# A weight sum behind the token sums, one store per quadrant and another order of the last products, in a linear attention and mixture-of-experts kernel

## The chip, the cores and the metric

The kernel runs on one core of one Trainium2 chip. The metric is the device time of one execution in microseconds (us). The core has five engines with a queue each: TensorE (PE in the profile), VectorE (DVE), ScalarE (ACT), GpSimd (POOL) and SyncE (SP, which only issues DMAs). ScalarE and GpSimd issue DMAs too. Each queue runs in order; the queues wait for one another by semaphores.

## The reference

Attention with a feature map phi replaces the softmax, for 8 samples, 8 heads, 576 tokens and 64 features per head. Its output, 4608 tokens of 512 features, goes through four experts whose outputs are added with a weight per token:

```python
kv = np.einsum('bhsd,bhse->bhde', k_p, v)
num = np.einsum('bhsd,bhde->bhse', q_p, kv)
...
for e in range(E):
    h = np.maximum(x @ w1[e], 0.0)
    out += p[:, e:e + 1] * (h @ w2[e])
```

Each expert has a first layer of 512 by 1024 and a second of 1024 by 512. The result is float32; the kernel multiplies in float16.

## The kernel before

**Tiles.** Tokens are worked on in nine tiles of 512. Tile j, from 0 to 7, is the first 512 tokens of sample j. The ninth tile, j = 8, holds the 64 tokens left over of each of the eight samples; its input is the tile `xT_left`. A unit is one tile and one expert; `81`, `82`, `83` in a name stand for tile 8 with experts 1, 2, 3.

**Products.** From tile 1 on, both layers use seven products in place of eight for a two-by-two block product (a Strassen scheme). It needs sums: of weights (`weight_sums`, `weight_sums2`, on VectorE, once per expert, lines 742 to 767), of input tokens (`token_sum`, on GpSimd, names `ts`, line 847) and of hidden values (`hidden_sum`, on GpSimd, names `hs`, lines 776 to 782). `t2.0` is `weight_sums2(2, 0)`, line 761: the difference of two blocks of the second-layer weights of expert 2, 128 partitions by 1024 elements. `t2.1` reads its result.

**A block of the first layer** (class `Block`) has the steps p1, p2, p6, p7, p5, c22, p4, p3. Products (line 866) go into the accumulators `b` and `e` in PSUM; ScalarE copies or applies ReLU (lines 877, 892, 899, 920); VectorE adds a copy and applies ReLU (`add_relu`, line 850).

**The second layer** (`layer2_product`, line 809) takes two halves of tokens (i = 0, 1) and seven products p. Each is four matmuls of 128 by 256. `m83.61` is product 6, second half, of tile 8 and expert 3. Products 1, 6, 7, 4 add up in one accumulator (`run`), 2, 5, 3 in another (`side`, which 2 and 5 start anew). After each product VectorE adds the accumulator, times the token's weight, into the float32 tile `acc` (`add_acc`, line 705), so the next product into the same accumulator waits for that add. For most units `run` and `side` are halves of a `py` bank; for the very last unit they are the banks `b` and `e`. In tile 0 the second layer is done plainly, in pieces y (line 714): `y2.33` is the last piece of expert 2 for the fourth group of 128 tokens.

**Stores.** An `acc` tile has 128 tokens by 512 features. For j < 8 SP stores it as one DMA (line 686). For the last tile, 64 of the 128 rows belong to each of two samples, whose rows lie 576 apart in DRAM. A quadrant (128 rows, 256 features) is stored as soon as it is done, after products 2, 7, 3 and 4, by two DMAs of 64 rows (line 692): one on SP's queue and one on ScalarE's, and for product 7, second half, both on GpSimd's.

**Order.** The order of all work is written out. Until about 100 us it is the list `EARLY` of names; each occurrence advances a step to its next `yield`. In the part around 70 us are `ts1.3` and `ts1.2` (token sums of tile 1), `b2.lkm` (line 385, two VectorE passes over left-over keys, tile `kz`), `b2.lq` (line 376 on ScalarE, which needs the PSUM that `b2.lkm` read) and `b1.load3` (an SP load). After `EARLY` each step has a position number, and steps run whole in order of it; the last unit's products use the order (1, 2, 6, 5, 7, 3, 4). At the end the order on TensorE is m82.70, .71, .40, .41, then m83.10, .11, .20, .21, .60, .61, .50, .51, .70, .71, .30, .31, .40, .41.

Of the kernel before, what the change touches and what calls it, by code (L numbers as in the profile page):

```python
# [80 lines left out]
    "KC": ('VV', 'VA', 'AA', 'AV'),  # L81
    "XT": ('AA', 'VV', 'VA', 'VV'),
    "CUT": (((0, 3, 4), (0, 3, 4), (0, 4), (0, 4)), ((0, 2, 4),) * 4),
    "WARM": (14, 5, 3, 1, 2, 1, 1),
    "BANK": {'qT0': 'b', 'qT1': 'py', 'kv2': 'py', 'qT2': 'py', 'kv3': 'b', 'nd10': 'b', 'nd10+': 'py', 'nd00': 'py', 'xT20': 'b', 'nd01': 'b', 'xT00': 'b', 'xT10': 'py', 'xT30': 'py', 'nd11': 'b', 'L20': 'b', 'xT11': 'b', 'L30': 'e', 'L10': 'e', 'L11': 'e', 'L00': 'py', 'L31': 'b', 'L01': 'e', 'L21': 'py', 'b1.lk': 'py', 'b1.q1': 'py', 'b1.q3': 'b', 'b1.q0': 'py', 'b1.nd10': 'b', 'b1.qT0': 'py', 'b1.nd00': 'b', 'b1.xT0': 'b', 'b1.xT3': 'py', 'b1.qTl': 'py', 'b1.nl': 'py'},
    "EARLY": (
# [12 lines left out]
        "p4.030 p2.031 b1.qT1 p6.031 p4.030 b1.nd21 w230 b1.qT0 b1.nd20 p7.031 c22.030 p5.031 b1.qT0 b1.nd00 b1.xT3 s3.2 b1.nd20 b1.nd01 b1.qT1 p3.030 b1.xT2",  # L99
        "b1.nd00 b1.nd10 b1.nd01 y2.20 b1.xT3 b1.nd11 y2.21 b2.ones p7.031 b1.xT2 b1.lq b1.xT0 y2.22 y2.23 b1.xT0 b1.nd10 b1.nd11 b1.xT1 b1.xT1 b2.load1 y2.02",  # L100
        "y2.03 ts1.0 b1.load4 b2.k0 p4.031 p4.031 b1.load1 p1.101 y2.30 p3.030 y2.23 p1.101 ts1.1 b2.lk c22.031 p3.031 y2.03 p1.100 b1.lqm y2.31 b1.qTl w231",
        "p1.100 p6.101 b1.qTl ts1.3 p3.031 b2.load0 y2.32 y2.33 b1.load3 t2.0 b2.lv p2.101 p6.100 p6.100 y2.33 b2.lkm y2.10 y2.11 t2.1 t0.1 b2.lq p2.100 p2.100",
        "y2.12 y2.13 b2.v0 p2.101 t3.0 b2.load5 p6.101 ts1.2 p7.100 y3.20 p7.100 b2.k3 y3.21 b2.v1 b2.load2 p5.100 p7.101 p7.101 b2.k1 b2.load3 y2.13 b1.nl",
        "y3.22 b2.km0 c22.100 b1.nl y3.23 b2.km3 y3.23 p3.100 p3.100 p4.100 b2.load9 p4.100 p5.101 b2.v2 b2.k2 b2.lqm y3.23 y3.10 y3.00 y3.01 p4.101 y3.02",
        "y3.03 p1.110 b2.km1 p4.101 hs10.00 t1.1 b2.v3 y3.11 p1.110 p6.110 c22.101 y3.03 b2.load4 b2.km2 p2.110 b2.kv p6.110 p2.110 y3.12 y3.13",
# [17 lines left out]
def kernel(  # L123
# [10 lines left out]
    nc = tc.nc  # L134
    ATTN, HSUM, L2ORD, L2AT = (CFG[x] for x in ("ATTN", "HSUM", "L2ORD", "L2AT"))

    B, H, S, D = q.shape
    N, E = moe_domain_probs.shape
    _, Dm, F = moe_w1.shape

    P = 128
    HP = P // 2
    CM = S // P
    SM = CM * P
# [67 lines left out]
    out_b = out.rearrange("(b s) d -> b s d", s=S)  # L212
# [467 lines left out]
    def new_py():  # L680
        return ppm.tile([P, Dm], FP32, tag="py", bufs=2, name="py")

    def store(j, ns, cols=slice(0, Dm), engs=(nc.sync, nc.scalar)):
        acc = accs[j, ns][:, cols]
        if j < B:
            nc.sync.dma_start(
                out=out_b[j, 0:SM].rearrange("(p c) d -> c p d", c=CM)[ns],
                in_=acc,
            )
        else:  # L690
            for u in range(2):
                engs[u].dma_start(
                    out=out_b[2 * ns + u, SM:S, cols],
                    in_=acc[u * HP : (u + 1) * HP],
                )

    def add_acc(j, e, ns, ps, ds, first):
        if (j, ns) not in accs:
            accs[j, ns] = pm.tile([P, Dm], FP32, tag="acc", bufs=NACC, name="acc")
        acc = accs[j, ns][:, ds]  # L700
        pscal = p_sb[:, j, ns, e : e + 1]
        if first:
            nc.scalar.activation(acc, ps, AF.Identity, scale=pscal)  # L703
        else:
            nc.vector.scalar_tensor_tensor(  # L705
                out=acc, in0=ps, scalar=pscal, in1=acc, op0=AO.mult, op1=AO.add
            )
# [76 lines left out]
    def layer2_product(j, e, hT, hss, p, i):  # L784


        if (j, e) == (NTILES - 1, E - 1):
            if p == 1:
                pys[j, e, i] = [ppm.tile([P, DH], FP32, tag=tag, bufs=2, name=f"p{tag}") for tag in ("b", "e")]
            run, side = pys[j, e, i]  # L790
        else:
            if p == 2:
                pys[j, e, i] = new_py()
            run, side = pys[j, e, i][:, 0:DH], pys[j, e, i][:, DH:Dm]
        ts = slice(i * P, (i + 1) * P)
        ts2 = slice(NH + i * P, NH + (i + 1) * P)
        w, tw = w2_sb[e], t2_sb[e]
        lo, hi = slice(0, FH), slice(FH, FC)
        ps, lhsT, rhs, first = {
            1: (run, lambda k: hT[k // 2][:, k % 2, 0, ts], w[:, lo, 0:DH], (j, e) == (NTILES - 1, E - 1)),  # L800
            2: (side, lambda k: hT[k // 2][:, k % 2, 1, ts], w[:, hi, 0:DH], True),
            5: (side, lambda k: hss[k // 2][0][:, k % 2, ts], tw[:, 0], True),
            6: (run, lambda k: hss[k // 2][1][:, k % 2, ts], tw[:, 1], False),
            7: (run, lambda k: hT[k // 2][:, k % 2, 0, ts2], w[:, lo, DH:Dm], False),
            3: (side, lambda k: hss[k // 2][3][:, k % 2, ts], w[:, hi, DH:Dm], False),
            4: (run, lambda k: hT[k // 2][:, k % 2, 1, ts2], tw[:, 2], False),
        }[p]
        for k in range(FH):
            nc.tensor.matmul(  # L809
                out=ps,  # L810
                lhsT=lhsT(k),
                rhs=rhs[:, k],
                start=first and k == 0,
                stop=k == FH - 1,
                skip_group_check=True,
            )
        yield
        c1, c2 = slice(0, DH), slice(DH, Dm)
        ns, ds, first = {
            2: (i, c1, True),  # L820
            5: (2 + i, c2, True),
            1: (i, c1, False),
            6: (i, c2, True),
            7: (2 + i, c2, False),
            3: (i, c2, False),
            4: (2 + i, c1, True),
        }[p]
        add_acc(j, e, ns, ps, ds, first and e == 0)
        if (j, e) == (NTILES - 1, E - 1):
            if p in (2, 3, 4, 7):  # L830
                yield
                store(j, ns, ds, *([(nc.gpsimd,) * 2] if (p, i) == (7, 1) else ()))
        elif e == E - 1 and p in (3, 4):
            yield
            store(j, ns)
# [164 lines left out]
    b0, b1 = bts[0], bts[1]  # L1000
    on = {"A": nc.scalar, "V": nc.vector, "P": nc.gpsimd, "S": nc.sync}
    with tc.manual_schedule(
# [5 lines left out]
        work = []  # L1008

        def put_at(pos, name, *g):  # L1010
            work.append((pos, len(work), name, g))
# [24 lines left out]
        NSLOT, LAG = 7, 6  # L1036

        def put_block(at, *g):
            bl = Block(*g)
            for pos, name in ((0, "p1"), (3, "p2"), (5, "p6"), (8, "p7"), (9, "p5"), (9.1, "c22"), (11, "p4"), (13, "p3")):  # L1040
                put_at(at + pos, f"{name}.{g[0]}{g[1]}{g[2]}", getattr(bl, name))
# [18 lines left out]
        for n, (j, e) in enumerate(units):  # L1060
            h, hss = [None, None], [[None] * 4, [None] * 4]
            at = base + 2 * NSLOT * n
            for d in range(2):
                put_block(at + d * NSLOT, j, e, d, h)
            at += 2 * NSLOT + LAG

            def hsum(d, i, hT=h, hss=hss):
                hidden_sum(hT[d], hss[d], i)

            for d in range(2):  # L1070
                for i in range(4):
                    put_at(at + HSUM[d][i], f"hs{j}{e}.{d}{i}", hsum, d, i)
            order = L2ORD
            if n == len(units) - 1:
                order, at = (1, 2, 6, 5, 7, 3, 4), at + NSLOT
            for m in range(14):
                put_at(at + L2AT[m], f"m{j}{e}.{order[m // 2]}{m % 2}", layer2_product, j, e, h, hss, order[m // 2], m % 2)

        for j in range(0, NTILES - 1):
            at = base + 2 * NSLOT * E * (j - 1) if j else 0.0  # L1080

            def put(pos, *g, at=at):
                put_at(at + pos, *g)

            if j + 1 < B:
                nxt = bts[j + 2] if j + 2 < B else None
                batch_steps(bts[j + 1], nxt, put, ATTN[j > 0], ATTN[1])
            else:
                put(CFG["LATE"][0], "b0.alloc", b0.alloc_left)
                put(CFG["LATE"][0], "b0.load", b0.load_left, "q")  # L1090
                put(CFG["LATE"][1], "b0.lq", b0.left_act, "q")
                put(CFG["LATE"][2], "b0.lqm", b0.left_dve, "q")
                put(CFG["LATE"][2] + 1, "b0.qTl", b0.dma_qTl)
                put(CFG["LATE"][3], "b0.nl", b0.nd_left)
            for i in range(4):
                if j:
                    put(2 * NSLOT * E + CFG["TSUM"][i], f"ts{j + 1}.{i}", token_sum, j + 1, i)
                else:
                    put(base + CFG["TSUM1"][i], f"ts1.{i}", token_sum, 1, i)
        work.sort(key=lambda w: w[0:2])  # L1100
        live = {name: g for _, _, name, g in work}
        assert len(live) == len(work)
# [45 lines left out]
```

## Time and profile before

| what | value |
|---|---|
| median of 3 runs | 491.01 us (491.0 to 491.03) |
| profiled execution | 491.24 us, its span 489.5 us |
| granted TensorE clock | 0.998 |
| HBM | 45.16 MB read, 9.44 MB written |
| second-layer matmul, 128x256 (L809) | one per 0.109 us, four in 0.44 us |
| add into acc, 128x256 (L705) | 0.48 us, one per 0.437 us in a row |
| hidden or token sum on GpSimd | 1.15 to 1.17 us |
| weight sum, 128x1024 (L761), four of them | 683, 688 (median) to 3419 ns |
| issue of a 64-row store on SP (L692) | 0.47 to 0.56 us |
| its landing after the issue | 1.9 to 2.6 us |

The span runs from the first to the last instruction in the trace; some 1.7 us lie around it. A line of the profile names the source line, the engine, what is written and read, the shapes, and how many instructions were merged. An idle time in brackets names what ended it. A queue's name with a q (SPq, ACTq) stands for the issuing of DMAs.

### The profile page before, as it was taken

Reading aid. Unit: us, or ns where it says so; the run is one execution under the profiler, and the core shown is the slowest. Engines: PE = TensorE matmul, PEld = TensorE weight load, DVE = VectorE, ACT = ScalarE, POOL = GpSimd, SP = SyncE. Lnnn points to the kernel's source line nnn. Section 1 sums busy time; section 2 is a strip of 40 time slices with the busy share of each in tenths; the row PEclk is TensorE's granted clock in tenths of the full one; section 3 lists DMA queues with packets and bytes.
Section 4 is the critical chain, followed back from the end, with each engine's and each line's share of the span. In section 5 each row is a group of like instructions: output and inputs, shape, how many; then the busy total and the mean of one; then the engine's idle time right before and its main releaser. Section 6 shows DMA issues by size and latency. Waiting matters only on the chain.

```text
span 489.5 us, 12007 instructions
## 1 busy us (share of the span) xinstructions
PE 477.5 (98%) x4567; PEld 407.8 (83%) x4567; DVE 382.2 (78%) x801; ACT 330.8 (68%) x656; POOL 358.3 (73%) x341
## 2 busy tenths in 40 slices
PE   7899998999999999999999999999999999999996
PEld 3676665898888988898889888988898888888885
DVE  5768999998958886788769885978687756775686
ACT  5489979855896498748884888478954565446530
POOL 4655044688967896789776976697769877987775
PEclk9999999999999999999999999999999999999999
DMA  8999968532445235524552345423131020002003
GB/s 280 199 226 262 249 127 243 154 94 47 134 154 122 50 112 190 113 60 113 171 128 65 95 144 145 92 56 119 56 76 28 5 95 1 2 0 88 2 1 86
DMA packets 81017, 53.67 MB, mean 110 GB/s; under 512 B 45152, under 2 KB 73696, under 8 KB 80960
## 3 DMA queue, kind: packets, MB, share of 16 engines
q1 hardware_dynamic: 70512, 41.05, 30.7%
q0 software_dynamic: 9888, 11.41, 12.3%
q8 instruction: 35, 0.57, 0.5%
q10 hardware_dynamic: 560, 0.46, 0.3%
q14 instruction: 22, 0.18, 0.1%
HBM read 45.16 MB, written 9.44 MB: 112 GB/s over the span
## 4 chain that ended last, share of the span: by engine, by line
PE 91%; ACT 3%; DVE 2%; DMA 1%; issue 1%; SPq 0%; DVEq 0%; ACTq 0%
PE py L809 39%; PE pb L866 24%; PE pe L866 18%; PE py L714 4%; PE ph L654 1%; PE psum_nd L471 1%; DMA kraws<-in_k_dram 1%; PE psum_kv L443 1%; DVE acc L705 1%; PE pb L809 1%; PE pe L809 0%; DVE t L761 0%; PE psum_nl L489 0%; ACT kp L343 0%; ACT u L877 0%
## 5 line engine op out<-in xcount | busy, mean ns | idle before, releaser
L705 DVE SCALAR_TENSOR_TENSOR acc<-py,p_sb,acc 128x256 f32<-128x256 f32 (+1 forms) x382 | 181.7, 488 | 43.1 <-PE py L809 37.3
L850 DVE CUSTOM_DVE_ANT_0 h<-pe,u 128x512 f16<-128x512 f32 x140 | 96.0, 687 | 46.8 <-PE pe L866 27.1
L866 PEld LDWEIGHTS <-w 128*128 128x128 f16 x1120 | 109.1, 98 | 17.4 <-issue 1.3
L776 POOL TENSOR_TENSOR hs<-h 128x512 f16<-128x512 f16 x64 | 73.9, 1154 | 59.4 <-DVE h L850 57.5
L809 PEld LDWEIGHTS <-h 128*128 128x128 f16 x1024 | 99.6, 98 | 12.7 <-issue 1.2
L809 PE MATMUL py<-w,h 128*128 128x256 f16 x744 | 106.4, 273 | 0.6 <-ACT acc L703 0.6
L877 ACT COPY u<-pb 128x512 f32<-128x512 f32 x140 | 82.5, 592 | 32.4 <-PE pb L866 29.7
L778 POOL TENSOR_TENSOR hs<-hs,h 128x512 f16<-128x512 f16 x64 | 75.0, 1173 | 26.4 <-PE py L809 24.0
L866 PEld LDWEIGHTS <-s 128*128 128x128 f16 x840 | 81.4, 98 | 12.1 <-issue 1.1
L866 PE MATMUL pb<-tt,w 128*128 128x256 f16 x560 | 83.7, 273 | 0.9 <-ACT u L877 0.9
L809 PEld LDWEIGHTS <-hs 128*128 128x128 f16 x768 | 74.4, 98 | 8.9 <-POOL hs L776 0.2
L782 POOL TENSOR_TENSOR hs<-h,hs 128x512 f16<-128x512 f16 x64 | 74.7, 1168 | 0.9 <-PE py L809 0.3
L780 POOL TENSOR_TENSOR h<-h 128x512 f16<-128x512 f16 x64 | 74.8, 1168 | 0.2
L809 PE MATMUL py<-t,hs 128*128 128x256 f16 x496 | 74.3, 273 | 0.0
L899 ACT ACTIVATE h<-pe 128x512 f16<-128x512 f32 x70 | 42.0, 600 | 44.1 <-PE pe L866 40.7
L892 ACT COPY pe<-pb 128x512 f32<-128x512 f32 x70 | 40.1, 574 | 38.6 <-PE pb L866 14.1
L920 ACT ACTIVATE h<-pb 128x512 f16<-128x512 f32 x70 | 42.0, 600 | 7.0 <-PE pb L866 7.0
L866 PE MATMUL pb<-tt,s 128*128 128x256 f16 x280 | 41.8, 272 | 0.6 <-ACT pe L892 0.6
L866 PE MATMUL pe<-tt,s 128*128 128x256 f16 x280 | 41.9, 273 | 0.0
L866 PE MATMUL pe<-xT,s 128*128 128x256 f16 x248 | 37.3, 273 | 0.0
L866 PE MATMUL pe<-xT,w 128*128 128x256 f16 x248 | 37.2, 273 | 0.0
L866 PE MATMUL pb<-xT,w 128*128 128x256 f16 x248 | 37.0, 273 | 0.0
(133 smaller groups left out, 598.7 us busy)
## 6 DMA issues: line engine op xcount, KB each, us to landing
out_dram<-acc SPq DMA_DIRECT2D x32, 256.0 KB, 2.5
w<-in_moe_w_dram POOLq DMA_DIRECT2D x14, 512.0 KB, 10.7
rawb<-in_k_dram SPq DMA_DIRECT2D x24, 256.0 KB, 3.3
rawb<-in_v_dram SPq DMA_DIRECT2D x24, 256.0 KB, 2.8
rawb<-in_q_dram SPq DMA_DIRECT2D x24, 256.0 KB, 2.7
rawq<-in_q_dram SPq DMA_DIRECT2D x4, 256.0 KB, 5.5
w<-in_moe_w_dram POOLq DMA_DIRECT2D x4, 256.0 KB, 6.1
rawb<-in_k_dram POOLq DMA_DIRECT2D x4, 256.0 KB, 8.6
```

What stands on the lines that cost most here:

```text
L705: nc.vector.scalar_tensor_tensor(out=acc, in0=ps, scalar=pscal, in1=acc, op0=AO.mult, op1=AO.add)
L776: nc.gpsimd.tensor_tensor(out=hs[0], in0=a21, in1=a22, op=AO.add)
L778: nc.gpsimd.tensor_tensor(out=hs[1], in0=hs[0], in1=a11, op=AO.subtract)
L780: nc.gpsimd.tensor_tensor(out=a21, in0=a11, in1=a21, op=AO.subtract)
L782: nc.gpsimd.tensor_tensor(out=hs[3], in0=a12, in1=hs[1], op=AO.subtract)
L809: nc.tensor.matmul(out=ps, lhsT=lhsT(k), rhs=rhs[:, k], start=first and k == 0, stop=k == FH - 1, skip_group_check=True,)
L850: nc.vector._custom_dve(TENSOR_ADD_SAT, out=out, in0=ps, in1=u, s0=BIG, s1=0.0)
L866: nc.tensor.matmul(out=ps[:, kk], lhsT=lk(kc), rhs=rhs[:, kc], start=first and kk == 0 and kc == 0, stop=kc == 1, skip_group_check=True,)
L877: nc.scalar.copy(u, self.b)
L892: nc.scalar.copy(self.e5, self.b)
L899: nc.scalar.activation(self.h[:, :, 0, 0:NH], self.e5, AF.Relu)
L920: nc.scalar.activation(self.h[:, :, 1, 0:NH], self.b, AF.Relu)
```

## The change

It has three parts. `t2.0` is placed some steps later in `EARLY`, behind the load, two casts, three product steps, the end of `y2.33` and `b2.lkm`. In the last tile a quadrant is stored by one DMA of 128 rows, on SP for the first half and on ScalarE for the second; its DRAM side is two samples of 64 rows. The last unit's products 5 and 6 change places, a table `MOVE` sets the positions of its products 1 and 2 to 512 (ahead of m82.40, at 512.8) and that of m82.41 to 528 (between m83.61, at 527.3, and m83.70, at 529.9).

```diff
+    "MOVE": {"m83.10": 512.0, "m83.11": 512.0, "m83.20": 512.0, "m83.21": 512.0, "m82.41": 528.0},
...
-        "p1.100 p6.101 b1.qTl ts1.3 p3.031 b2.load0 y2.32 y2.33 b1.load3 t2.0 b2.lv p2.101 p6.100 p6.100 y2.33 b2.lkm y2.10 y2.11 t2.1 t0.1 b2.lq p2.100 p2.100",
+        "p1.100 p6.101 b1.qTl ts1.3 p3.031 b2.load0 y2.32 y2.33 b1.load3 b2.lv p2.101 p6.100 p6.100 y2.33 b2.lkm t2.0 y2.10 y2.11 t2.1 t0.1 b2.lq p2.100 p2.100",
...
-    def store(j, ns, cols=slice(0, Dm), engs=(nc.sync, nc.scalar)):
+    def store(j, ns, cols=slice(0, Dm), eng=nc.sync):
         acc = accs[j, ns][:, cols]
...
         else:
-            for u in range(2):
-                engs[u].dma_start(
-                    out=out_b[2 * ns + u, SM:S, cols],
-                    in_=acc[u * HP : (u + 1) * HP],
-                )
+            eng.dma_start(
+                out=out_b[2 * ns : 2 * ns + 2, SM:S, cols],
+                in_=acc,
+            )
...
         if (j, e) == (NTILES - 1, E - 1):
             if p in (2, 3, 4, 7):
                 yield
-                store(j, ns, ds, *([(nc.gpsimd,) * 2] if (p, i) == (7, 1) else ()))
+                store(j, ns, ds, nc.sync if i == 0 else nc.scalar)
...
             if n == len(units) - 1:
-                order, at = (1, 2, 6, 5, 7, 3, 4), at + NSLOT
+                order, at = (1, 2, 5, 6, 7, 3, 4), at + NSLOT
...
+        work = [(CFG["MOVE"].get(w[2], w[0]), *w[1:]) for w in work]
         work.sort(key=lambda w: w[0:2])
```

## The prediction

> **What bounds the kernel now.** I read the page first, its engine shares and the chain that ended last.
>
> ```profile
> PE 477.5 (98%) x4567; PEld 407.8 (83%) x4567; DVE 382.2 (78%) x801; ACT 330.8 (68%) x656; POOL 358.3 (73%) x341
> PE 91%; ACT 3%; DVE 2%; DMA 1%; issue 1%; SPq 0%; DVEq 0%; ACTq 0%
> ```
>
> TensorE is busy for 98% of the span and makes 91% of the chain. A gain must be a stall of TensorE taken away, or something after its last matmul. So next the waits of TensorE from 60 us to the end (waiting line, releaser, us in total, times, longest), and around the first of them the timelines (start, length, what).
>
> ```profile
> PE pb L866 <- ACT u L877: 0.9, 1, 0.9
> PE pb L866 <- ACT pe L892: 0.6, 1, 0.6
> PE py L809 <- DVE acc L705: 0.3, 1, 0.3
> ...
> 68.52 3.42 DVE L761 TENSOR_TENSOR t<-w 128x1024 f16<-128x1024 f16 x1
> 71.86 0.74 DVE L705 SCALAR_TENSOR_TENSOR acc<-py,p_sb,acc 128x512 f32<-128x512 f32 x1
> 72.52 0.84 DVE L385 SCALAR_TENSOR_TENSOR kz<-kz,psum_el 64x256 f16<-64x256 f16 x2
> 74.60 0.68 DVE L761 TENSOR_TENSOR t<-w 128x1024 f16<-128x1024 f16 x1
> ...
> 69.10 1.17 POOL L847 TENSOR_TENSOR tt<-xT,tt 128x512 f16<-128x512 f16 x1
> 70.22 1.16 POOL L847 TENSOR_TENSOR tt<-xT 128x512 f16<-128x512 f16 x1
> ...
> 73.45 0.39 ACT L376 ACTIVATE psum_el<-rl 128x256 f32<-128x256 f32 x1 [1.49 <-DVE kz L385]
> ```
>
> The weight sum t2.0 takes 3.42 us at 68.52; the same form takes 0.68 at 74.60. It ends at 71.94, 0.56 after GpSimd's last token sum (71.38). What queues behind it on VectorE is late: ScalarE waits 1.49 for kz, its later copies come late, and TensorE stalls for 0.88 at 75.0 and for 0.65 at 82.35.
>
> Last, the tail: the end of the chain, the store issues, and the DMA slices from 478 us on (40 slices of 0.29 us).
>
> ```profile
> 477.94 1.03 PE py L809 x8
> 483.38 2.23 DVE acc L705 x5
> ...
> 485.53 1.20 SPq L692 DMA_DIRECT2D out_dram<-acc  x2
> 486.47 0.55 ACTq L692 DMA_DIRECT2D out_dram<-acc  x1
> ...
> GB/s 0 0 0 0 0 0 0 0 0 0 0 0 0 0 167 232 189 221 104 0 0 0 25 192 221 232 104 143 392 185 310 271 235 218 203 7 0 0 0 0
> q10 hardware_dynamic: 560, 0.46, 14.6%
> out_dram<-acc ACTq DMA_DIRECT2D x7, 64.0 KB, 2.3
> ```
>
> VectorE's last add ends at 483.38 + 2.23 = 485.61, but ScalarE's queue issues the last half store only at 486.47, because each issue holds a queue for 0.55. Packets flow until about 488.1; the span ends 1.4 later. 560 packets in 7 stores are 80 each: 64 rows, and 16 of a few bytes that count the landing.
>
> **Part 1, t2.0 moved.** It goes behind the add of y2.33 and the two kz passes on VectorE; it issues no DMA, and on the queues of SP, GpSimd and ScalarE nothing changes place. VectorE is then free at 68.60. The matmuls of y2.33 start at 69.12 and take 1.03, so the add starts at 70.17 instead of 71.86, kz 0.66 later (as 71.86 to 72.52), and t2.0 0.84 after that, at 71.67, when GpSimd's sums are over by 0.3. With 0.69 for it, t2.1, which reads it, starts at 72.39 instead of 73.39: **1.0 us earlier**, not 2.7, as 1.5 us of VectorE now passes waiting for TensorE. If it met a GpSimd sum again it would lose up to 2.7 and everything behind it would be late. ScalarE's kz wait ends 1.49 sooner, but its exponential at 76.72 waits for VectorE's pass at 75.98, which moves by 1.0; from there ScalarE runs without a gap to its copy at 82.31, which releases TensorE at 83.00. So the first stall goes and TensorE is 1.0 ahead at 83.00. ScalarE's casts on the way read loads whose slowest landing there is 7.8 after the issue: the one issued at 69.34 is in by 77.1, before its cast at 77.2. Bounds: 0 (a landing holds ScalarE as before) to 1.53 (both stalls); taken: 1.0, the step that ends last. TensorE has one stall of 0.57 and one of 0.30 after that, both relative to its own work, so the 1.0 reaches the end.
>
> **Part 2, last products.** Products 1 and 2 of the last unit (four products of 4 matmuls, 0.44 each) move ahead of m82.40; m82.41 goes between products 6 and 7; 5 goes ahead of 6. TensorE's 0.30 wait before 477.94 is m82.40 waiting for the add of m82.70 on its accumulator; m83.10 in that place has free banks. VectorE's adds then run without a gap from 477.41, one per 0.437: 18 of them end at 477.41 + 17 x 0.437 + 0.48 = 485.32 instead of 485.61. Product 5 stands three products behind 2, product 7 three behind 6, so each accumulator's add is over as its next product comes (by 0.0 to 0.1). GpSimd's sums end, by its timeline, at 479.28, 480.51, 481.62 and 482.74; products 5, 6, 7, 3 need them at 479.9, 480.8, 482.1 and 483.0. Gain **0.3**; bounds 0 to 0.5.
>
> **Part 3, stores.** Eight quadrants of 128 rows by 1 KB. Sixteen issues become eight, four on SP and four on ScalarE, none on GpSimd. The last one is issued 0.03 after its add, not 0.86: 0.83 sooner. Landing is 2.3 for 64 rows, and the page gives 2.5 for 128 rows of 2 KB: 0.6 to 0.8 gained, if the transfer is spread as those are.
>
> That is what no row shows. All transfers of this kernel have 64 or 128 as their outermost count on both sides, also the loads with a count of 2 or 4 inside it, and each spreads into 16 equal shares (4 or 8 rows of that count). The new store has 128 partitions on the SBUF side, but on the DRAM side an outermost count of **2** (two samples, 576 rows apart, which can't be merged) with 64 rows inside. Shares of the outermost count, as in all rows, would be one each for two engines: 64 packets of 1 KB per engine and store. Shares of the total would be 8 rows for each of 16. Of the price of a 1 KB packet: the fullest slice, 392 GB/s, is 24.5 GB/s per engine, 42 ns; the queue's 14.6% of 16 x 11.5 us over its 448 rows is 60 ns, the small packets and the waiting of two queues on one engine included. I take 46, near the busy end.
>
> The Trainium skill ("DMA: Bandwidth & Descriptors", section "Why a DMA increments its semaphore by 16 and not by 1") says that a DMA runs on the largest number of engines up to 16 that divides the slowest dimension above 1 of both sides; that is two here, and the sum would be the 506 below. The same page's "Rules for kernel authors" advises one 128-partition transfer in place of two halves; by that alone the sum would be 489.0. No run here shows an outermost count under 16.
>
> With two engines: the first store is issued as the fifth add ends, 477.41 + 4 x 0.437 + 0.48 = 479.64, less 1.0 from part 1; packets start 1.2 later (480.84 to the fifteenth slice, 482.03), at 479.87. Eight stores are 512 packets per engine, 512 x 0.046 = 23.6 us; the first two alone last to 485.8, and the third is issued at 482.1, so the engines never run dry. They end at 503.4, the span 1.4 later, at 504.8. Of the gains of parts 1 and 2 only this is left: the first store is issued at 478.67 instead of 480.84.
>
> **Sum.** The profiled execution took 491.24 with a span of 489.5; the runs' median is 491.01. Span +15.3, so 491.0 + 15.3 = **506.3 us**; 42 ns give 504.3, 60 ns give 513.5. This case's own range is 503 to 513.5.
>
> **The rivals.**
> *Spread over 16 engines (faster).* Place: the eight stores; price: 1.0 + 0.3 + 0.75 = 2.05, so 489.0 (488.2 to 490.3). For it: every 128-row transfer here lands in 2 to 4 us. Against: each of them has its large count outermost. It decides from six engines on: 8 x 128 / 6 x 0.046 = 7.9 us from 479.87 ends at 487.7, before the 488.1 of now.
> *Spread, but t2.0 is slow wherever it stands.* If the 3.42 us is not GpSimd's doing, t2.0 from 71.67 delays t2.1 to 75.1, 1.7 late: +1.7 - 1.05 gives 491.7; with half of it, 491. Against: the other three of its form took 0.68 to 0.69, with no GpSimd work beside them.
> *Two engines and a slower packet.* One engine alone for each half may find less overlap; at 71 ns (175 GB/s at a share of 0.76, 482.0 to 483.5) 512 packets take 36 us: 519.
>
> **Chances.** From the rows alone, equal shares of the outermost count fit every transfer and shares of the total need the issuer to split a run across a count, which no row does: 0.78 for two engines at 42 to 60 ns, 0.02 for the slower packet, 0.17 for the spread with all gains, 0.03 for the spread with t2.0 slow. A measurement here tells 0.2%, 1.0 us, from no change: faster 0.17, same 0.03 (491.7 is within it), slower 0.80. The range must reach the fast case to leave out under 2 in 10: 488.2 to 513.5.
>
> **What would show it.** Two engines: eight store issues of 128 KB with landings of 7 to 20 us, some 45 GB/s for 23 us after TensorE's last matmul (slices at an eighth of the DMA share), VectorE's last add near 484.3. Part 1: L761 four times at 0.69, no wait of TensorE for u at 75, its wait for pe near 82 kept or longer. Part 2: no wait of L809 for acc near 477. The forecast is wrong if the stores land in 2 to 3 us; the time is then 489.

## The result and the profile after

The changed kernel takes 506.63 us (median of 6 runs, 506.17 to 508.16) against 491.01 before: 1.0318 times as long, 95% interval 1.0299 to 1.0336. The prediction was 506.3, or 1.0311. The profiled execution took 506.87 us with a span of 505.1.

The page of the changed kernel, engine shares and chain:

```profile
PE 477.9 (95%) x4567; PEld 408.3 (81%) x4567; DVE 379.1 (75%) x801; ACT 331.2 (66%) x656; POOL 357.2 (71%) x339
PE 89%; DMA 3%; DVE 1%; ACT 1%; POOL 0%; issue 0%; SPq 0%; ACTq 0%
```

TensorE is busy for as long as before (477.9 against 477.5 us); its share falls because the span is 15.6 longer. VectorE has 3.1 us less work; 2.7 of it is t2.0 (0.69 us instead of 3.42), which no longer stands beside GpSimd's sums. The time must lie behind the matmuls, so the next views are the tail of VectorE and the DMA slices from 478 us to the end (40 slices of 0.69 us).

```profile
484.08 0.92 DVE L705 SCALAR_TENSOR_TENSOR acc<-pb,p_sb,acc 128x256 f32<-128x256 f32 x2
...
GB/s 0 0 0 7 28 36 34 48 40 46 46 51 46 48 36 49 48 49 48 49 48 48 49 48 49 48 48 49 48 48 49 48 49 48 49 48 45 0 0 0
q10 hardware_dynamic: 520, 0.52, 5.5%
out_dram<-acc SPq DMA_DIRECT2D x4, 128.0 KB
...
L692 SPq DMA_DIRECT2D out_dram<-acc x4: 511/601/4580, 479.4 to 484.6; - x4
L692 ACTq DMA_DIRECT2D out_dram<-acc x4: 527/1034/5264, 479.8 to 485.2; - x4
```

VectorE's last add ends at 485.00, 0.6 earlier than before. From then on nothing computes. The stores flow for 23 us, from 480 to 503, at 28 to 51 GB/s and in most slices at 48, where the full slices of before had 104 to 392. A queue's 520 packets in four stores are 130 each: 128 rows and 2 that count the landing, where the 64-row stores of before had 16 of these. In the trace the semaphore of each store is written three times, once at the issue and twice as data land; the landings come 5.8 us after the issue for the first store and 18.6 for the last. So each store ran on two DMA engines, which the runs below test. The last lines (issue times on the two queues, shortest/median/longest in ns) show that the last issue on either queue was held for 4.6 and 5.3 us, while earlier stores of these queues had not landed.

The stretch of t2.0, as in the prediction: TensorE's waits from 60 us on, VectorE, and TensorE's first longer wait.

```profile
PE py L714 <- DMA w<-in_moe_w_dram: 1.1, 1, 1.1
PE py L809 <- ACT acc L703: 0.6, 2, 0.4
PE pb L866 <- ACT pe L892: 0.2, 1, 0.2
...
70.25 0.75 DVE L705 SCALAR_TENSOR_TENSOR acc<-py,p_sb,acc 128x512 f32<-128x512 f32 x1 [1.59 <-PE py L714]
70.92 0.84 DVE L386 SCALAR_TENSOR_TENSOR kz<-kz,psum_el 64x256 f16<-64x256 f16 x2
71.79 0.69 DVE L761 TENSOR_TENSOR t<-w 128x1024 f16<-128x1024 f16 x1
72.52 1.29 DVE L763 TENSOR_TENSOR t<-w,t 128x1024 f16<-128x1024 f16 x2
...
76.79 1.02 PE L714 MATMUL py<-w,h 128*128 128x512 f16 x4 [1.14 <-DMA w<-in_moe_w_dram]
```

t2.0 takes 0.69, starts after an idle time of 1.59 and the steps named, and t2.1 starts at 72.52 instead of 73.39. The old wait for u is gone, and a wait of 1.14 for weights is there instead.

### The profile page after: what moved, and what is told of

Same layout as the page of the kernel before. It is cut to its first block, busy times and chain, and to the rows that moved or that the text cites. A ratio compares the mean times of both kernels' runs of the same rounds, so it can differ in the third digit from the quotient of the medians.

```text
span 505.1 us, 11996 instructions
## 1 busy us (share of the span) xinstructions
PE 477.9 (95%) x4567; PEld 408.3 (81%) x4567; DVE 379.1 (75%) x801; ACT 331.2 (66%) x656; POOL 357.2 (71%) x339
## 4 chain that ended last, share of the span: by engine, by line
PE 89%; DMA 3%; DVE 1%; ACT 1%; POOL 0%; issue 0%; SPq 0%; ACTq 0%
PE py L809 37%; PE pb L866 23%; PE pe L866 18%; PE py L714 4%; DMA w<-in_moe_w_dram 2%; PE ph L655 1%; PE psum_nd L472 1%; PE psum_kv L444 1%; DMA kraws<-in_k_dram 1%; DMA out_dram<-acc 1%; PE pb L809 1%; PE warm_ps L995 1%; PE pe L809 1%; POOL tt L847 0%; DVE acc L705 0%; PE psum_kv L606 0%
```

## The experiments

Each run is compared with runs of the kernel before on the same chip; their medians there were 491.2 to 491.4, with single executions from 489.9 to 493.4.

**Which part makes it slower.** First the changed kernel with the stores of before:

```diff
-            eng.dma_start(
-                out=out_b[2 * ns : 2 * ns + 2, SM:S, cols],
-                in_=acc,
-            )
+            for u in range(2):
+                engs[u].dma_start(
+                    out=out_b[2 * ns + u, SM:S, cols],
+                    in_=acc[u * HP : (u + 1) * HP],
+                )
```

> The changed kernel with its stores put back to two 64-row halves (seven on each of two queues, two on GpSimd's); t2.0 and the last products stay as changed. Theory (the stores alone make the kernel slower): the last add of VectorE ends at 485.0 as in the changed kernel's trace, 0.6 ahead of before, and the rest is as before: 490.4 us. Rival (the new order of the products, or t2.0, has a part in the loss): over 491.2.

> The changed kernel with the stores of before once more, for a profile of an undisturbed execution. Theory: TensorE waits for the second half of expert 3's weights near 76 whenever these land over 7.3 us after their issue, VectorE's adds of the tail run without a gap, the end is 0.86 behind the last add as before: 490.4 us. Rival (part 2 gains nothing): 490.8.

Measured 490.47 against 491.38, ratio 0.9982 (0.9967 to 0.9997), and in the second run 490.24 against 491.18, ratio 0.9981 (0.9965 to 0.9996): 0.9 us faster than before. So the two other parts have no share in the loss. The waits of TensorE in the second run:

```profile
PE py L715 <- DMA w<-in_moe_w_dram: 1.0, 1, 1.0
PE py L810 <- ACT acc L704: 0.7, 2, 0.5
PE pb L867 <- ACT pe L893: 0.2, 1, 0.2
```

The wait for the weights is that of the changed kernel; the wait of the second layer for VectorE's add (0.3 before) is gone.

Then the reverse, the kernel before with the new stores and nothing else:

> The kernel before with the one-DMA stores alone. Theory (eight stores are 512 packets of 1 KB on each of two engines, and these run dry nowhere): the first store is issued at 480.84 instead of 479.35, so the end is 1.5 later than the changed kernel's, 506.6 + 1.5 = 508.1 us. Rival (the loss comes from how much the other two parts crowd the tail): well under 506.

Measured 507.76 against 491.38, ratio 1.0334 (1.0298 to 1.0369). The expectation of 508.1 is within it. In the traces the first store is issued at 480.39 here and at 479.35 in the changed kernel, and the spans are 506.1 and 505.1: the other two parts change the loss by no more than the 1.0 us by which they bring the first store forward.

**What about the stores.** The two counts of the DRAM side change places:

```diff
-                out=out_b[2 * ns : 2 * ns + 2, SM:S, cols],
+                out=out_b[2 * ns : 2 * ns + 2, SM:S, cols].rearrange("u r d -> r u d"),
```

> The changed kernel with the two counts of a store's DRAM side exchanged: 64 rows outermost, 2 samples inside. Bytes, packets, queues and number of issues stay; the rows of a quadrant land at other rows of the same two samples, so the output is not the reference's in the last tile. Theory (the outermost count, 2, sets the number of engines): 16 engines, landings of 2 to 3 us, 490.4 less up to 0.8 for the shorter queue: 489.6 to 490.0 us. Rival (a transfer of 128 rows over two samples is slow whatever the order): 506 to 507.

Measured 489.51 against 491.38, ratio 0.9963 (0.9949 to 0.9977). Its DMA view from 478 to 490 us (slices of 0.30 us):

```profile
GB/s 0 0 0 0 55 335 249 236 0 0 0 0 0 0 0 0 246 284 331 335 232 328 341 256 270 0 0 0 0 0 0 0 0 0 0 0 0 0 0 0
q10 hardware_dynamic: 576, 0.52, 12.9%
out_dram<-acc SPq DMA_DIRECT2D x4, 128.0 KB, 2.1
out_dram<-acc ACTq DMA_DIRECT2D x4, 128.0 KB, 2.1
```

576 packets in four stores are 144 each: 128 rows and 16 that count the landing. The same bytes on the same queues, in as many issues, land in 2.1 us at some 300 GB/s. Only the order of the counts differs, so neither 128 rows in one transfer nor rows of two samples in it is slow. So the cause is the small outermost count, and this run shows it.

A count between 2 and 16 is the next test. The 64-row stores of before, with 4 outermost:

```diff
-                    out=out_b[2 * ns + u, SM:S, cols],
+                    out=out_b[2 * ns + u, SM:S, cols].rearrange("(r a) d -> a r d", a=4),
```

> The kernel with parts 1 and 2 and the 64-row stores of before, whose DRAM side is written with 4 as the outermost count and 16 rows inside; rows of the last tile land permuted within their 64, so its output is not the reference's. Theory (the outermost count is the number of engines): 14 stores of 16 packets on each of four engines of the two hardware queues, 224 x 45 ns = 10.1 us from 480.4, the end 1.5 later: 493.5 to 495 us. Rival (the loss came from 128 rows in one transfer): 490.4.

Measured 496.4 against 491.18, ratio 1.0106 (1.0080 to 1.0132). The slices of its DMA view from 478 to 495 us (0.43 us each):

```profile
GB/s 0 0 0 0 0 14 60 92 60 77 77 94 96 63 63 94 67 99 63 46 58 119 137 63 46 70 80 82 94 96 96 96 96 96 96 68 12 0 0 0
```

At full load it is 96 GB/s, twice the 48 of the changed kernel: 24 GB/s for each engine in both. The rival, 490.4, is out. The time is 1.4 us over the upper end expected: the sum counted 45 ns for every row, which is too little. In the trace a row takes 46 ns from 490 us on, but 54 on average until 485.5. And from 485.5 to 487.0, where the slices fall to 46, GpSimd's two stores (q0) are under way, and the two hardware queues move 23 packets, where 150 of q1 and 149 of q10 go in the 3 us from 490:

```profile
q0 software_dynamic: 43, 0.07, 37.9%
q1 hardware_dynamic: 11, 0.01, 5.6%
q10 hardware_dynamic: 12, 0.01, 2.6%
```

Why the other stores slow down so much beside GpSimd's was not tested. In the trace each of these hardware-queue stores has five updates of its semaphore, one at the issue and four as data land.

**Where the gain of t2.0 went.** The kernel before with t2.0 moved alone:

> The kernel before with t2.0 moved and nothing else. Theory (the gain is taken back by TensorE's wait for the second half of expert 3's weights, which lands at 76.75): 0.15 to 0.2 us, 490.8. Rival (the prediction's step: 1.0 us reaches the end): 490.0.

Measured 490.77 against 491.38, ratio 0.9987 (0.9973 to 1.0001): 0.6 us; the interval holds the expected 0.2 and the prediction's 1.0 alike. Its waits of TensorE, and its VectorE:

```profile
PE pb L866 <- ACT pe L892: 0.7, 1, 0.7
PE py L809 <- ACT acc L703: 0.6, 1, 0.6
PE py L809 <- DVE acc L705: 0.3, 1, 0.3
...
68.60 0.69 DVE L850 CUSTOM_DVE_ANT_0 h<-pe,u 128x512 f16<-128x512 f32 x1 [0.49 <-PE pe L866]
72.42 0.69 DVE L761 TENSOR_TENSOR t<-w 128x1024 f16<-128x1024 f16 x1
```

In this execution there is no wait for weights. Counted from the same step of VectorE ahead of t2.0 (67.91 before, 67.97 changed, 68.60 here), TensorE passes the place of its second stall at 83.00 - 67.91 = 15.09 before, 82.81 - 67.97 = 14.84 in the changed kernel and 82.75 - 68.60 = 14.15 here. The move is worth 0.94 us here and 0.25 there. The difference is the landing of the second half of expert 3's weights: 7.1 us after its issue here, 8.4 in the changed kernel and 8.2 before. TensorE now asks for them 1.1 us earlier; before, they landed at 76.51 and the matmuls that read them started at 76.55, so nothing was to spare.

So that load was moved forward, ahead of the memset on GpSimd's queue that waits until 65 us:

```diff
-        "b1.nd00 b1.nd10 b1.nd01 y2.20 b1.xT3 b1.nd11 y2.21 b2.ones p7.031 ...
+        "b1.nd00 b1.nd10 b1.nd01 y2.20 b1.xT3 b1.nd11 y2.21 w231 b2.ones p7.031 ...
-        "y2.03 ts1.0 ... b1.lqm y2.31 b1.qTl w231",
+        "y2.03 ts1.0 ... b1.lqm y2.31 b1.qTl",
```

> Parts 1 and 2 with the stores of before, and the load of the second half of expert 3's weights moved ahead of the memset on GpSimd's queue that waits until 65 us; it is issued near 47 us then. Theory (the landing of these weights takes back the gain of t2.0): no wait of TensorE for w at 76, 0.7 us faster than the same kernel without it: 489.7. Rival (the earlier load delays the others of that stretch, up to 65 us): 491 or more.

> The kernel with parts 1 and 2, the stores of before and the early load, once more, beside the interleaved one on the same chip: 1.5 us faster than before.

Measured 489.66 against 491.18, ratio 0.9965 (0.9952 to 0.9977), and 490.36 against 491.35, ratio 0.9971 (0.9956 to 0.9985). In the first run the only wait of TensorE after 60 us is

```profile
PE pb L867 <- ACT pe L893: 0.8, 2, 0.4
```

The wait for weights is gone in both. Counted as above, TensorE passes the second stall at 14.70 with parts 1 and 2 and the stores of before, and at 14.30 and 14.11 with the load moved: 0.4 and 0.6 us sooner in the traces, 0.8 and 1.0 sooner than before. In the times it is not clear of noise: the medians give 0.6 us in the first run (489.66 against 490.24) and 0.1 in the second (1.0 against 0.9 faster than before), and the intervals overlap. The second run fell short of its 1.5 us by 0.5.

**The last products alone.** The kernel before with the new order and positions:

> The kernel before with the new order of the last products alone (stores and t2.0 as before). Theory: TensorE's stall ahead of m82.40 goes (matmuls 0.47 us apart more than their pace in the trace of before), and the last add ends that much sooner: 0.45 us faster than before. The prediction's size: 0.3. Rival (an accumulator's add holds TensorE elsewhere): 0 to 0.1.

Measured 490.82 against 491.35, ratio 0.9986 (0.9973 to 0.9999): 0.5 us, as expected, though the interval holds 0.3 and the rival's 0.1 too. The trace decides: it has no wait for VectorE's add in the tail, and from the last ReLU of VectorE to the end of its last add there are 8.34 us, against 8.80 before, which is 0.46.

**Better stores.** GpSimd issues a later pair of the half stores:

```diff
-                store(j, ns, ds, *([(nc.gpsimd,) * 2] if (p, i) == (7, 1) else ()))
+                store(j, ns, ds, *([(nc.gpsimd,) * 2] if (p, i) == (3, 1) else ()))
```

> Parts 1 and 2 with the 64-row stores of before; GpSimd issues those of product 3's second half instead of product 7's. Theory (half stores keep 16 engines, and what cost 0.86 us at the end was only that the queues were still issuing): the last issue starts 0.1 to 0.2 after the last add, 0.7 us faster than with the stores of before: 489.7. Rival (GpSimd's slower issue ends last): 490.4 or more.

Measured 491.27 against 491.18, ratio 1.0003 (0.9988 to 1.0018): the theory fell. GpSimd and the landing times, in two views:

```profile
484.54 1.12 POOL L693 DMA_DIRECT2D out_dram<-acc  x2 [1.82 <-DVE acc L706]
...
DMA to landing us min/median/max: 2.0/2.3/2.9
```

GpSimd's two stores are issued until 485.66. In the trace, its drain, an instruction at the program's end, lasts to 489.20, 0.6 after SP is done at 488.61. The last three landings on the two queues take 2.6 to 2.9 us, against 2.0 to 2.3 with the stores of before, and the last issue on ScalarE still starts 0.64 after the last add, not 0.1 to 0.2. From the last add to the end of the span there are 4.88 us, against 3.87 with the stores of before: what is saved on the two queues is more than given back.

Last, a kernel with everything that helped, and with one store per quadrant that puts each row in its place. The last tile's tokens are interleaved, so that 64 rows can be outermost:

```diff
+    def left_cols(b):
+        return xT_left.rearrange("p c (n r u) -> p c n r u", r=SL, u=2)[:, :, b // 2, :, b % 2]
...
-                out=t[u * HP : (u + 1) * HP, B],
+                out=t[u : P : 2, B],
...
+        def xl_copy(self):
+            nc.scalar.copy(out=left_cols(self.b), in_=self.xs)
```

> A kernel with all that the runs point to: parts 1 and 2, the weights of expert 3 loaded early, and one store per quadrant whose DRAM side has 64 rows outermost; the last tile's tokens are interleaved (row r of the one sample beside row r of the other) by a ScalarE copy per sample, so that this is the right place for each row. Theory: 1.7 us for the stores and order as in the run with rows outermost, 0.6 for the weights: 2.3 to 2.5 us faster than before, 0.7 faster than with early weights alone. Rival (eight more copies on ScalarE or the interleaved load of the token weights cost it): no faster than with early weights alone.

Measured 489.99 against 491.35, ratio 0.9969 (0.9956 to 0.9983). That is 1.4 us faster than before, not the 2.3 to 2.5 expected, and no clear gain over the kernel with early weights alone (0.9971 on the same chip, the same runs of before; the intervals overlap). Its waits, and two lines of ScalarE, with the same copy in the kernel with early weights alone (second run) below them:

```profile
PE pb L873 <- ACT pe L899: 0.6, 1, 0.6
PE pb L873 <- ACT u L884: 0.4, 1, 0.4
PE py L816 <- ACT acc L710: 0.2, 1, 0.2
...
124.36 0.48 ACT L514 COPY xT_left<-xTs 128x256 f16<-128x256 f16 x1 [0.95 <-DMA xTs<-x_sl]
124.71 0.57 ACT L884 COPY u<-pb 128x512 f32<-128x512 f32 x1
...
123.23 0.62 ACT L878 COPY u<-pb 128x512 f32<-128x512 f32 x1
```

TensorE waits 0.4 for a ScalarE copy, in the trace at 125 us. No such wait is there with early weights alone. The first interleaving copy (L514) causes it: ScalarE's queue stands still for 0.95 until the transposed tokens have landed, so the copy behind it that TensorE needs starts at 124.71 instead of 123.23. The tail gained what the stores promised: 3.38 us from the last add to the end of the span, against 3.86 with early weights alone.

## Why the prediction was right, and where its steps were off

**The stores, the deciding step.** Right in mechanism and size. The order of the two counts alone moves the changed kernel's time between 506.6 and 489.5, and 2, 4 and 64 outermost give 48, 96 and some 300 GB/s. The packet was put at 46 ns; 48 GB/s over two engines is 1,024 bytes in 43 ns at full load, and in the trace the 22.9 us from the first row (480.6) to the end of the last (503.5) are 45 ns for each of 512. The prediction's 0.78 for this case came from rows that could not show it; that the outermost count sets the number of engines was an inference until these runs.

The Trainium skill ("DMA: Bandwidth & Descriptors", section "Why a DMA increments its semaphore by 16 and not by 1") gives the number of engines as the largest up to 16 that divides the slowest dimension of both sides; the runs agree at 2, 4 and 16. It also says that the issuer writes the rest of the 16 itself at once, which fits the three updates of a store on two engines and the five on four. Its advice in "Rules for kernel authors", one 128-partition transfer for two halves, holds with rows outermost (a landing of 2.1 us) and cost 16.4 us here without, in the run with the new stores alone (507.76 against 491.38).

**Part 1, t2.0.** Right on VectorE: t2.1 came 0.93 us earlier in the profile (73.39 - 67.91 against 72.52 - 67.97) where 1.0 was predicted, and t2.0 took 0.69. Wrong on TensorE. The step "the first stall goes and TensorE is 1.0 ahead" looked only at ScalarE's loads and left out that TensorE itself reads weights still in flight there: they landed at 76.51 before, 0.04 ahead of the matmuls that the stall of 0.88 had made late, and at 76.75 now. Of 1.0 predicted, 0.25 reached the place of the second stall in the changed kernel's profile. This was small beside the stores. It fits that parts 1 and 2 together gave 0.9 us and not 1.3, though the intervals of these runs hold 1.3 too.

The prediction's check of ScalarE's loads paired the wrong two. In the trace the load issued at 69.34 landed at 76.99 and was first read at 78.22, by an exponential; the cast at 77.24 read the load issued at 68.84, in by 74.58. Read 1.0 earlier, the load of 69.34 would have had 0.2 to spare, and that is what it had (in by 77.14 and read at 77.34 in the changed kernel). It went well by a small margin that the check did not show.

**Part 2, the last products.** Right that the 0.30 wait goes and that no new one comes; the size, 0.3, was too small, within its bounds of 0 to 0.5. From the last ReLU of VectorE (476.81 before, 476.66 now) to the end of its last add there were 8.80 us and are 8.34: 0.46 instead of 0.3. The wait was read as 0.30, but by TensorE's starts it cost more: the matmuls at 477.94 start 1.33 after the eight at 476.61, where eight take 0.87 without a wait, so 0.46 was lost. And the term "one per 0.437" was TensorE's pace. Freed of waiting, VectorE's adds come every 0.39 (477.27 to 478.05 for two), so it catches up what the prediction took as fixed.

**The rival.** With the stores spread over 16 engines it forecast 489.0, a gain of 2.05; the kernel with rows outermost took 489.51 on a chip where the kernel before took 491.38, a gain of 1.87. From the last add to the end of the span that kernel needs 3.40 us (483.79 to 487.19) and the one before 3.85: one issue per quadrant is worth 0.45, where the rival had 0.75.

**The place in time.** The first store was issued at 479.35 instead of 478.67, as part 1 gave less, and the first row moved at 480.6 instead of 479.9. The rows then took 22.9 us instead of 23.6, so they ended at 503.5, where 503.4 was predicted: two errors of 0.7 cancelled, and that the total came within 0.3 us was partly luck. The span ended at 505.1 instead of 504.8.

## What to carry to other kernels

Two transfers joined into one are cheaper to issue, but look at the outermost count of both sides: with 2 and 4 outermost the transfers here ran on two and four DMA engines, and the swap of two counts in the pattern was worth 17 us, more than anything done on the compute engines. When a stall is taken away, ask what else the stalled engine reads: a load whose landing the stall covered becomes the next wait. And at the end of a program count each queue's last issue, landing and drain, not only the last arithmetic.

## What the runs showed of the hardware

A DMA engine moved 1 KB rows from SBUF to HBM at 24 GB/s at full load, as one of two (48 GB/s) and as one of four (96 GB/s). An issue that takes 0.55 us with 16 engines took 4.6 on SP and 5.3 on ScalarE as the fourth store of its queue on two engines, while earlier ones had not landed.

The VectorE weight sum that took 3.42 us beside GpSimd did not get in between two GpSimd sums that followed each other directly (69.10 to 71.38): it ended 0.56 after the second. Alone it takes 0.68 to 0.69, in all four places of the changed kernel.

With GpSimd's last store issued until 485.66, 0.5 after the last add, the program ended late through GpSimd's drain: 489.20 against 488.61 for SP. In the kernel before, whose GpSimd stores are issued until 485.27, the two ended together (488.66 and 488.69).
